# Products of the first thirteen blocks kept in a ring of four buffers, and the diagonal placed with a raised priority

## The chip, the cores and the metric

The kernel runs on one core of a Trainium2 chip. The metric is the time of one execution on the device in microseconds; the kernel before was run three times.

## The reference

A linear attention with a decaying state feeds two feed-forward layers. For every step t of 768, per batch (4) and head (8, of width 48):

```python
for t in range(S):
    kt, vt, rt = (k[:, :, t], v[:, :, t], r[:, :, t])
    cur = np.einsum('bhd,bhe->bhde', u[None] * kt, vt)
    y[:, :, t] = np.einsum('bhd,bhde->bhe', rt, state + cur)
    state = w[None, :, :, None] * state + np.einsum('bhd,bhe->bhde', kt, vt)
...
h = (x @ w1) * (x @ w2) @ w3          # first layer: x is 3072 x 384, inner width 1024
x = h @ w_out
h = x @ w_in                          # second layer: inner width 2048
return (h * np.cos(h)) @ w_out2
```

## The kernel before

The attention is done in 12 chunks of 64 steps. For chunk c and each half g of the heads, PE makes the scores `sc` (L518, L521), DVE puts them into the tile `am` under a strict mask (`mask_scores`, L533), ACT copies `am` into `xa` and `xb` (L539, L540), and PE multiplies these with the values to get `y` (L554) and the next state `st` (L591). ACT evacuates `y` to `yt` (L556); PE transposes it (`xp`, L569), and ACT and DVE split it into a high and a low half (`xh`, `xl`). Before the masks, DVE puts a diagonal into the same `am`: it forms the sums `dg` (L478, L480, L481) and places them with one predicated copy of 128x1024 (`prep_g`, L505). The scores of a chunk need its two operands `rd` and `kd`, which SP loads (L367) when the scores of the chunk before are done, and which DVE then scales in place (L486).

The first layer runs beside the attention. `ab(j, m)` makes, for a block of 512 tokens and 128 columns, `a = x @ w1` and `b = x @ w2`, each from nine products of high and low halves (`mm3`, L273 to L275). ACT copies `a` into an SBUF tile `p` (L772), DVE multiplies it by `b` (L773), and the POOL queue stores the product to DRAM, `pd` (L774); it is read back later. `a` and `b` lie in a ring of three PSUM banks, `p` in a ring of two SBUF buffers under the tag `p`. So the copy for a block waits until the store of an earlier block has left its buffer.

Another ring, tag `stg`, has four buffers of the same size. Its first user is `hot`, the operand of the filler products `hps` (L409) that stop before the 35th microsecond. The next ones are the pieces of w3 that `fold_load` splits (two buffers for each pair of steps, with `FOLD` from block 14 on), later the staged x2 and the output.

The weights come as 64-bit numbers; `decode` turns them into high and low halves on DVE (L313, L316, L319, L332) and ACT (L330).

A scheduler orders the instructions of each engine by priority, by data and by when a buffer comes free. The order is fixed when the program is built, and each engine then runs its own list in that order. `tc.high_priority(offset=40)` puts what stands under it 40 places ahead; the masks have it in `att_mask`, and the copy and the multiplication of `p` have -80.

```python
BUFS = {"wx": 4, "wf": 4, "p": 2, "ph": 3, "pl": 3, "stg": 4, "raw": 2, "dt": 1}
ORDER = [(j, m) for j, a, b in ((0, 0, 6), (1, 0, 4), (0, 6, 8), (1, 4, 8)) for m in range(a, b)]
FOLD = [0] * 14 + [1, 1, 1, 0] * 8 + [0] * 2
```

Of the kernel before, what the change touches and what calls it, by code (L numbers as in the profile page):

```python
# [184 lines left out]
def kernel(  # L185
# [19 lines left out]
    with ExitStack() as own:  # L205
        held = own.enter_context(tc.tile_pool(name="held", bufs=1))
        dram = own.enter_context(tc.tile_pool(name="slow", bufs=1, space=DRAM))
        flag = held.tile([1, 1], I32, name="flag")
        chunked(
            tc, flag, rd_in, kd_in, rt_in, kt_in, vt_in, wT_in, u_in, w1_in, w2_in, w3T_in, wo_in, wi2_in, wo2_in, out  # L210
        )
        odd = nc.values_load(flag[0:1, 0:1], min_val=0, max_val=48)
        with tc.If(odd > 0):
            xc = dram.tile([out.shape[0], 384, 512], F32, name="xc")
            sequential(tc, rt_in, kt_in, vt_in, w_in, u_in, xc)
            plain(tc, xc, w1_in, w2_in, w3T_in, wo_in, wi2_in, wo2_in, out)
# [3 lines left out]
def chunked(  # L220
# [41 lines left out]
    def kt_(tag, shape, nm, dt=F32):  # L262
        return keep.tile(list(shape), dt, tag=tag, name=nm, bufs=BUFS[tag])

    def bank(nm, tag):
        return psum.tile([128, 512], F32, tag=tag, name=nm, bufs={"ab": 3, "att": 2, "acc": 3}[tag])
# [5 lines left out]
    def mm3(o, wh, wl, xh, xl, first, last):  # L272
        nc.tensor.matmul(o, wh, xh, start=first, stop=False)  # L273
        nc.tensor.matmul(o, wh, xl, start=False, stop=False)  # L274
        nc.tensor.matmul(o, wl, xh, start=False, stop=last)  # L275
# [7 lines left out]
    def flush():  # L283
        while late:
            late.pop(0)()
# [204 lines left out]
    def masked(c):  # L490
        return ((ams[c], 0, 128),)
# [9 lines left out]
            nc.scalar.copy(zb[0:64], kt[0:64])  # L501

    def prep_g(c):
        for x, o, e in masked(c):
            nc.vector.copy_predicated(  # L505
                out=x[o:e].rearrange("p g h t -> p (g h) t"),
                mask=mdiag[o:e].unsqueeze(1).to_broadcast([e - o, 2 * H, C]),
                data=dg[o:e].unsqueeze(2).to_broadcast([e - o, 2 * H, C]),
            )
# [87 lines left out]
    halves, whole = [slice(0, 256), slice(256, 512)], slice(0, 512)  # L597
# [6 lines left out]
    def att_slot(c, i):  # L604
        if c >= NSTEP:
            return
        n = c + 1 if c + 1 < NSTEP else None
        if i == 0:
            att_scores(c)
            att_mask(c)  # L610
            loads(c + 1)
        elif i == 1:
            att_y(c, 0)
            att_state(c, 0)
            if n:
                prep_d(n)
        elif i == 2:
            att_y(c, 1)
            att_x(c, 0)
            att_state(c, 1)  # L620
            if n:
                load_v(n)
                prep_u(n)
        else:
            att_x(c, 1)
            if n:
                prep_z(n)
                prep_g(n)
# [10 lines left out]
    def w12(m, n):  # L639
        g, i = divmod(m, 4)  # L640
        fs = slice(i * 128, (i + n) * 128)
        for which, hi, lo in ((1, w1h, w1l), (2, w2h, w2l)):
            if g not in hi:
                hi[g] = wp.tile([128, 3, 512], F32R, tag=f"g{g}", bufs=4, name=f"w{which}h{g}")
                lo[g] = wp.tile([128, 3, 512], F32R, tag=f"g{g}", bufs=4, name=f"w{which}l{g}")
            decode(w12_id[which, m], (hi[g][:, :, fs], lo[g][:, :, fs]))
# [6 lines left out]
    for ps in range(3):  # L653
        n = 128 * min(3, NM1 - 3 * ps)
# [42 lines left out]
    def fold_step(n):  # L697
        for _ in range(n):
            if folds:
                it = folds.pop(0)  # L700
                fold_load(*it)
                fold_pend.append(it)
            if len(fold_pend) > (2 if folds else 0):
                if not folds:
                    flush()
                fold_mm(*fold_pend.pop(0))
# [48 lines left out]
                nc.scalar.copy(s, acc[j][e])  # L755
                nc.sync.dma_start(out=x2d[j][:, e, :], in_=s)

    def ab(j, m, cols=slice(0, 512)):
        g, i = divmod(m, 4)
        fs = slice(i * 128, (i + 1) * 128)  # L760
        n = cols.stop - cols.start
        a = bank(f"a{j}_{m}", "ab")[:, 0:n]
        b = bank(f"b{j}_{m}", "ab")[:, 0:n]
        for t, wh, wl in ((a, w1h, w1l), (b, w2h, w2l)):
            for kk in range(3):
                mm3(
                    t, wh[g][:, kk, fs], wl[g][:, kk, fs], xh[j][:, kk, cols], xl[j][:, kk, cols], kk == 0, kk == 2
                )
        p = kt_("p", (128, 512), f"p{j}_{m}")[:, 0:n]

        with tc.high_priority(offset=-80):
            nc.scalar.copy(p, a)  # L772
            nc.vector.tensor_tensor(out=p, in0=p, in1=b, op=ALU.mult)  # L773
        nc.gpsimd.dma_start(out=pd[j][m][:, cols], in_=p)  # L774
# [28 lines left out]
    load_v(1)  # L803
    prep_u(0)
    prep_g(0)
    att_mask(0)
    warm(24)
# [10 lines left out]
    decays()  # L818
    flush()
    ab(0, 0, halves[0])  # L820
    prep_u(1)
    prep_g(1)
    prep_z(1)
    att_mask(1)
# [5 lines left out]
    att_state(1, 0)  # L830
    flush()
    ab(0, 1, halves[0])
    att_x(1, 1)
    att_state(1, 1)
# [11 lines left out]
    def advance(n):  # L846
        for _ in range(n):
            att_slot(*next(slots, (NSTEP, 0)))

    for i, (j, m) in enumerate(ORDER):  # L850
        advance(SLOTS[i])
        if i in (1, 6):
            w12({1: 4, 6: 6}[i], 2)
        fold_step(FOLD[i])
        flush()
        ab(j, m, halves[1] if j == 0 and m < 2 else whole)
    while folds or fold_pend:
        fold_step(1)
    att_cm.__exit__(None, None, None)
# [16 lines left out]
    for i in range(NBLK * NM1):  # L876
        j, m = divmod(i, NM1)
# [64 lines left out]
    for it in items + [None] * 5:  # L942
        if it:
            j, m = it
# [80 lines left out]
```

## Time and profile before

| | us |
|---|---|
| median of three runs | 863.75 |
| the three runs | 861.83, 863.75, 864.93 |
| the profiled execution, its own time | 865.14 |
| its span (first to last instruction) | 863.4 |
| PE busy in the span | 840.5 (97%) |
| DVE busy | 554.8 (64%) |
| ACT busy | 415.6 (48%) |

The execution has 1.74 us outside of its span. PE is the busiest engine; how its idle time lies in the span is told by the waits and by the busy times in stretches. A granted clock of 1.00 is full speed, 2.4 GHz, and 0.50 is 1.2 GHz.

### The profile page before, as it was taken

The page shows a single profiled execution, that of the slowest core. Times are in us where ns is not written, and L with a number is a line of the kernel's source. Part 1 is how long each engine was busy: PE and PEld are TensorE (multiplying, and loading weights), DVE is VectorE, ACT ScalarE, POOL GpSimd, SP SyncE. Part 2 cuts the span into 40 slices and gives each one's busy share as a digit, 9 for nine tenths or more (in the row PEclk, how much of TensorE's full clock was granted, in tenths as well). Part 3 has the DMA queues.
Part 4 walks back from the last instruction along what each step waited for, and adds up shares of the span by engine and source line. Part 5 has one row for each costly group of instructions (what it writes and reads, how often), then busy time and mean ns, then how long its engine had stood idle before and what let it go on. Part 6 is the DMA issues. An engine that isn't in the chain of part 4 may idle for free.

```text
span 863.4 us, 14166 instructions
## 1 busy us (share of the span) xinstructions
PE 840.5 (97%) x5630; PEld 682.9 (79%) x5634; DVE 554.8 (64%) x839; ACT 415.6 (48%) x708; POOL 35.9 (4%) x66
## 2 busy tenths in 40 slices
PE   6987999999999999999999999999999999999997
PEld 3775778888888888888888888888888888888885
DVE  8876977786555534498956655655655655655552
ACT  4764555544553531255446445445545544544442
POOL 3000010010100001000000000000000000000000
PEclk9988999999999999999999999999999999999998
DMA  8757566565343263288952002001001100100101
GB/s 254 208 182 221 163 199 210 177 206 151 113 149 110 71 209 132 90 305 296 326 177 74 1 1 73 1 1 59 15 1 38 36 0 15 59 0 1 38 1 40
DMA packets 41161, 95.04 MB, mean 110 GB/s; under 512 B 4736, under 2 KB 6400, under 8 KB 41088
## 3 DMA queue, kind: packets, MB, share of 16 engines
q1 hardware_dynamic: 37072, 81.28, 30.0%
q0 software_dynamic: 3872, 12.59, 3.9%
q8 instruction: 46, 0.75, 0.4%
q10 hardware_dynamic: 144, 0.20, 0.1%
q14 instruction: 27, 0.22, 0.1%
HBM read 72.03 MB, written 22.02 MB: 109 GB/s over the span
## 4 chain that ended last, share of the span: by engine, by line
PE 94%; DVE 2%; DMA 1%; ACT 1%; issue 1%; ACTq 0%; DVEq 0%
PE p L274 12%; PE p L273 12%; PE p L275 12%; PE h L275 8%; PE h L273 8%; PE h L274 8%; PE a L273 4%; PE b L273 4%; PE b L275 4%; PE b L274 4%; PE a L274 4%; PE a L275 4%; PE y L554 3%; PE sc L518 2%; PE hps L409 2%; PE st L591 2%
## 5 line engine op out<-in xcount | busy, mean ns | idle before, releaser
L921 ACT ACTIVATE u<-h,qbias 128x512 f32<-128x512 f32 x96 | 66.2, 689 | 138.0 <-PE h L275 138.0
L922 DVE TENSOR_SCALAR n<-u 128x512 f32<-128x512 f32 x96 | 41.1, 428 | 138.0 <-ACT u L921 138.0
L275 PE MATMUL h<-x2h,wil 128*128 128x512 f32 x288 | 113.2, 393 | 0.0
L273 PE MATMUL h<-x2h,wih 128*128 128x512 f32 x288 | 113.1, 393 | 0.0
L274 PE MATMUL p<-gl,woh 128*128 128x512 f32 x288 | 113.1, 393 | 0.0
L274 PE MATMUL h<-x2l,wih 128*128 128x512 f32 x288 | 113.0, 392 | 0.0
L275 PE MATMUL p<-gh,wol 128*128 128x512 f32 x288 | 113.0, 392 | 0.0
L273 PE MATMUL p<-gh,woh 128*128 128x512 f32 x288 | 113.0, 392 | 0.0
L924 ACT ACTIVATE u<-n 128x512 f32<-128x512 f32 x96 | 60.9, 634 | 65.1 <-DVE n L923 65.1
L930 DVE TENSOR_TENSOR u<-u,h 128x512 f32<-128x512 f32 x96 | 66.0, 687 | 16.7 <-ACT u L924 16.7
L773 DVE TENSOR_TENSOR p<-p,b 128x512 f32<-128x512 f32 (+1 forms) x50 | 33.1, 661 | 62.4 <-PE b L275 35.7
L923 DVE SCALAR_TENSOR_TENSOR n<-n,u 128x512 f32<-128x512 f32 x96 | 66.4, 692 | 3.3
L936 DVE TENSOR_TENSOR gl<-u,gh 128x512 fp32r<-128x512 f32 x96 | 65.7, 685 | 0.7 <-ACT gh L932 0.7
L274 PEld LDWEIGHTS p<-gl,woh 128*128 128x128 f32 x288 | 54.1, 188 | 12.4
L275 PEld LDWEIGHTS h<-x2h,wil 128*128 128x128 f32 x288 | 54.1, 188 | 12.3
L273 PEld LDWEIGHTS h<-x2h,wih 128*128 128x128 f32 x288 | 54.1, 188 | 12.3
L274 PEld LDWEIGHTS h<-x2l,wih 128*128 128x128 f32 x288 | 54.1, 188 | 12.2
L273 PEld LDWEIGHTS p<-gh,woh 128*128 128x128 f32 x288 | 54.1, 188 | 12.2
L275 PEld LDWEIGHTS p<-gh,wol 128*128 128x128 f32 x288 | 54.1, 188 | 12.2
L772 ACT COPY p<-a 128x512 f32<-128x512 f32 (+1 forms) x50 | 28.3, 568 | 67.3 <-PE a L275 56.0
L273 PE MATMUL a<-xh,w1h 128*128 128x512 f32 (+1 forms) x150 | 60.4, 403 | 0.0
L932 ACT CAST gh<-u 128x512 fp32r<-128x512 f32 x96 | 58.9, 613 | 0.8 <-DVE u L930 0.8
(163 smaller groups left out, 1717.5 us busy)
## 6 DMA issues: line engine op xcount, KB each, us to landing
pr<-pd SPq DMA_DIRECT2D x48, 256.0 KB, 4.1
pd<-p POOLq DMA_DIRECT2D x46, 256.0 KB, 2.8
raw<-in_wo_dram SPq DMA_DIRECT2D x12, 768.0 KB, 5.0
raw<-in_w3T_dram SPq DMA_DIRECT2D x8, 768.0 KB, 5.0
raw<-in_wi_dram SPq DMA_DIRECT2D x8, 768.0 KB, 5.6
raw<-in_w_dram SPq DMA_DIRECT2D x6, 768.0 KB, 5.7
x2d<-x SPq DMA_DIRECT2D x18, 256.0 KB, 5.5
x2s<-x2d SPq DMA_DIRECT2D x18, 256.0 KB, 3.3
```

What stands on the lines that cost most here:

```text
L273: nc.tensor.matmul(o, wh, xh, start=first, stop=False)
L274: nc.tensor.matmul(o, wh, xl, start=False, stop=False)
L275: nc.tensor.matmul(o, wl, xh, start=False, stop=last)
L772: nc.scalar.copy(p, a)
L773: nc.vector.tensor_tensor(out=p, in0=p, in1=b, op=ALU.mult)
L921: head[0] = nc.scalar.activation(out=u, in_=h, func=AF.Identity, scale=INV_2PI, bias=qbias).ins
L922: nc.vector.tensor_scalar_add(out=n, in0=u, scalar1=RND)
L923: nc.vector.scalar_tensor_tensor(out=n, in0=n, scalar=RND, in1=u, op0=ALU.subtract, op1=ALU.subtract)
L924: nc.scalar.activation(out=u, in_=n, func=AF.Sin, scale=-TWO_PI)
L930: nc.vector.tensor_tensor(out=u, in0=u, in1=h, op=ALU.mult)
L932: nc.scalar.copy(gh, u)
L936: nc.vector.tensor_tensor(out=gl, in0=u, in1=gh.bitcast(F32), op=ALU.subtract)
```

## The change

The diagonal's placement gets the priority that the masks behind it have, and the products of the half blocks ahead of the loop and of the loop's first 13 blocks (i from 0 to 12) are kept in the ring `stg` and no more in `p`.

```diff
     def prep_g(c):
+        with tc.high_priority(offset=40):
+            place_diagonal(c)
+
+    def place_diagonal(c):
         for x, o, e in masked(c):
             nc.vector.copy_predicated(
...
-    def ab(j, m, cols=slice(0, 512)):
+    def ab(j, m, cols=slice(0, 512), early=True):
...
-        p = kt_("p", (128, 512), f"p{j}_{m}")[:, 0:n]
+        p = kt_("stg" if early else "p", (128, 512), f"p{j}_{m}")[:, 0:n]
...
-        ab(j, m, halves[1] if j == 0 and m < 2 else whole)
+        ab(j, m, halves[1] if j == 0 and m < 2 else whole, early=i < 13)
```

No instruction is added or left out. What moves is the order on PE, DVE, ACT and SP; on POOL nothing moves. In the names below, `y2_0` is the y of chunk 2, first half of the heads, `b0_1` the b of block j = 0, m = 1; a number behind that is the buffer's. Line numbers of the changed kernel are four higher from `prep_g`'s body on.

On DVE, where chunk 2 is prepared, the kernel before has:

```order
L496 TENSOR_TENSOR kt_130<-kt_130,tk0_139 128x768
L332 TENSOR_TENSOR w1l0_362<-dt4_678,w1h0_361 128x3x256
L505 COPY_PREDICATED am_133<-mdiag_143,dg_144 128x1024
L313 TENSOR_SCALAR dt5_686<-raw5_593 128x768
L533 COPY_PREDICATED am_133<-mstrict_142,sc2_0_705 128x512
L316 SCALAR_TENSOR_TENSOR dt5_686<-raw5_593,dt5_686 128x768
L533 COPY_PREDICATED am_133<-mstrict_142,sc2_1_722 128x512
```

And the changed kernel:

```order
L496 TENSOR_TENSOR kt_130<-kt_130,tk0_139 128x768
L509 COPY_PREDICATED am_133<-mdiag_143,dg_144 128x1024
L332 TENSOR_TENSOR w1l0_362<-dt4_678,w1h0_361 128x3x256
L537 COPY_PREDICATED am_133<-mstrict_142,sc2_0_705 128x512
L313 TENSOR_SCALAR dt5_686<-raw5_593 128x768
L537 COPY_PREDICATED am_133<-mstrict_142,sc2_1_722 128x512
L316 SCALAR_TENSOR_TENSOR dt5_686<-raw5_593,dt5_686 128x768
```

The diagonal has passed the low half of w1, and each of the two masks one step of the next decoding.

On PE at the same place, the changed kernel has the end of `a0_1`, then the nine products of `b0_1`, and then `y2_0` (in the kernel before, `b0_1` stands behind the 32 products of `y2_0` and `st2_0`, 32 rows further on):

```order
L275 MATMUL a0_1_835<-xh0_380,w1l0_362 128x256
L273 MATMUL b0_1_836<-xh0_380,w2h0_370 128x256
L274 MATMUL b0_1_836<-xl0_381,w2h0_370 128x256
L275 MATMUL b0_1_836<-xh0_380,w2l0_371 128x256
...
L558 MATMUL y2_0_775<-va_134,xa_131 64x48
L595 MATMUL st2_0_794<-va_134,za_136 48x48
L558 MATMUL y2_0_775<-vb_135,xb_132 64x48
```

So PE has nine products to do where it stood before `y2_0`.

On ACT, where chunk 3 is worked on, the kernel before has:

```order
L500 COPY za_136<-kt_130 64x768
L501 COPY zb_137<-kt_130 64x768
L539 COPY xa_131<-am_133 64x512
L540 COPY xb_132<-am_133 64x512
L539 COPY xa_131<-am_133 64x512
L540 COPY xb_132<-am_133 64x512
L772 COPY p0_4_1076<-a0_4_1056 128x512
L556 COPY yt3_0_1033<-y3_0_1016 128x384
```

And the changed kernel:

```order
L776 COPY p0_4_1076<-a0_4_1056 128x512
L500 COPY za_136<-kt_130 64x768
L501 COPY zb_137<-kt_130 64x768
L543 COPY xa_131<-am_133 64x512
L544 COPY xb_132<-am_133 64x512
L543 COPY xa_131<-am_133 64x512
L544 COPY xb_132<-am_133 64x512
L560 COPY yt3_0_1033<-y3_0_1016 128x384
```

The copy of the product `p0_4` no more stands between the masked scores and the evacuation of `y3_0`.

On PE, a little later, the changed kernel has the scores of chunk 4 behind the first product of `a1_0` and of `b1_0` (before, behind all of `a1_0`, `b1_0`, `a1_1` and `b1_1`):

```order
L573 MATMUL xp3_1_1129<-ident_141,yt3_1_1097 128x128 x3
L273 MATMUL b0_5_1142<-xh0_380,w2h1_824 128x512
L274 MATMUL b0_5_1142<-xl0_381,w2h1_824 128x512
L275 MATMUL b0_5_1142<-xh0_380,w2l1_825 128x512
L273 MATMUL a1_0_1181<-xh1_878,w1h0_361 128x512
L273 MATMUL b1_0_1182<-xh1_878,w2h0_370 128x512
L522 MATMUL sc4_0_1229<-rd_127,kd_128 64x64
L525 MATMUL sc4_0_1229<-rd_127,kd_128 64x64
```

The scores of chunk 4 have passed 34 products of the first layer.

## Rows read from the trace of the kernel before

**Rows 1.** Busy time by stretch: length, engines' busy us, PE clock, DMA share, GB/s.

```profile
48.20:51.00 2.80, 0.03 (x1) 0.03 (x1) 2.80 (x5) 1.31 (x3) 0.00 (x0) 0.84 1.05 307
51.00:57.00 6.00, 5.80 (x75) 5.33 (x75) 6.00 (x10) 3.85 (x7) 1.08 (x2) 0.51 0.63 187
57.00:78.20 21.20, 20.91 (x253) 16.07 (x252) 16.49 (x22) 11.54 (x18) 1.62 (x3) 1.00 0.68 203
78.20:83.60 5.40, 0.06 (x3) 0.03 (x2) 1.66 (x2) 1.05 (x3) 0.00 (x0) 0.74 0.87 294
83.60:88.00 4.40, 4.40 (x56) 3.56 (x58) 1.35 (x3) 3.48 (x6) 0.54 (x1) 0.54 0.18 67
88.00:111.00 23.00, 23.00 (x177) 18.72 (x172) 21.53 (x27) 10.28 (x16) 2.16 (x4) 1.00 0.65 184
111.00:857.00 746.00, 746.00 (x4495) 610.33 (x4493) 462.55 (x709) 353.44 (x596) 21.77 (x39) 1.00 0.29 96
```

**Rows 2.** Waits of PE, 20 to 120 us: total, times, longest.

```profile
PE y L554 <- ACT yt L556: 5.3, 1, 5.3
PE y L554 <- DMA rd<-in_rd_dram: 2.8, 1, 2.8
```

**Rows 3.** Chain that ended last: start, us, what.

```profile
73.99 8.48 DMA pd<-p
...
83.57 1.95 PE y L554 x32
...
111.54 1.07 PE y L554 x32
112.61 0.72 PE st L591 x32
...
122.99 0.48 PE xp L569 x3
```

**Rows 4.** ACT in order of time: start, us, form; in brackets idle before, releaser.

```profile
50.30 0.61 ACT L539 COPY xa<-am 64x512 f32<-64x512 f32 x1 [1.47 <-DVE am L533]
50.95 0.62 ACT L540 COPY xb<-am 64x512 f32<-64x512 f32 x1
...
82.55 0.58 ACT L772 COPY p<-a 128x512 f32<-128x512 f32 x1 [5.57 <-DMA pd<-p]
83.03 0.48 ACT L556 COPY yt<-y 128x384 f32<-128x384 f32 x1
```

**Rows 5.** DVE in order of time.

```profile
46.99 0.95 DVE L332 TENSOR_TENSOR w1l<-dt,w1h 128x768 fp32r<-128x768 f32 x1
47.86 1.29 DVE L505 COPY_PREDICATED am<-mdiag,dg 128x1024 f32<-128x1024 uint8 x1
49.04 0.55 DVE L313 TENSOR_SCALAR dt<-raw 128x768 uint32<-128x768 uint32 x1
49.50 0.71 DVE L533 COPY_PREDICATED am<-mstrict,sc 128x512 f32<-128x512 uint8 x1
...
79.66 1.23 DVE L486 TENSOR_TENSOR rd<-rd,t 128x1024 f32<-128x1024 f32 x1 [1.68 <-DMA rd<-in_rd_dram]
```

**Rows 6.** PE in order of time.

```profile
51.62 0.34 PE L554 MATMUL y<-vb,xb 112*64 112x48 f32 x1 [0.20 <-ACT xb L540]
...
89.58 0.39 PE L273 MATMUL a<-xh,w1h 128*128 128x512 f32 x1
...
98.67 0.40 PE L273 MATMUL b<-xh,w2h 128*128 128x512 f32 x1
```

**Rows 7.** POOL's issue of the third store of a product.

```profile
55.49 0.54 POOL L774 DMA_DIRECT2D pd<-p  x1 [1.78 <-DVE p L773]
```

**Rows 8.** The loads of rd: SP's issue, their landing, and the median of all.

```profile
71.94 0.79 SPq L367 DMA_DIRECT2D rd<-in_rd_dram  x2
...
DMA to landing us min/median/max: 6.4/6.8/7.2
...
rd<-in_rd_dram SPq DMA_DIRECT2D x20, 192.0 KB, 4.4
```

## The prediction

> **What bounds the kernel now.** I read the busy times by stretch first, then PE's waits, then the chain of waits backwards, and last the lists of ACT and DVE at the two places that the waits name. The stretches [rows 1] show that from 111 to 857 us PE is busy for 746.00 of 746.00 us at a clock of 1.00: whatever PE gets done earlier before 111 us arrives whole at the end, and nothing else does. Ahead of that, two stretches are nearly empty, 48.2 to 51 (0.03 us busy) and 78.2 to 83.6 (0.06), and behind each lies one at about half clock (0.51 and 0.54). PE's waits name them [rows 2]: 2.8 us and 5.3 us, both before products `y`.
>
> The longer one ends in the chain with 8.48 us of a store `pd` issued at 73.99, and PE's `y` starts at 83.57 [rows 3]. ACT tells why [rows 4]: at 82.55 it copies a product after 5.57 us of waiting for that store, and the evacuation `yt`, for which PE waits, is the next one in its list, at 83.03. The `y` that it evacuates was done long before. So a two-buffer ring of products stops the attention, only because ACT works in order.
>
> The shorter one is put down to a load of `rd`. But ACT's copies into `xa` and `xb` at 50.30 and 50.95 wait for DVE's mask [rows 4], and DVE works without a pause there: it is busy 2.80 of 2.80 us [rows 1]. So DVE's order is the cause: the diagonal starts only at 47.86, behind a low half of w1 at 46.99, and the mask at 49.50, behind a decoding step at 49.04 [rows 5].
>
> **The change, part by part.** The sum is made against the profiled execution: 863.4 us of span and 1.74 around it, 865.14.
>
> *The first pause.* With the diagonal first, DVE goes diagonal, low half, mask. The diagonal starts at 46.99; it takes 49.04 - 47.86 = 1.18 to the next start, the low half 47.86 - 46.99 = 0.87, so the first mask starts at 49.04 and no more at 49.50 [rows 5]. `xb` and then the run of `y` products follow 0.46 us earlier: 51.16 for 51.62 [rows 6]. What is late next is that copy again. In the pause PE now also has the nine products of `b0_1`, which it did later before; 39 products of 512 columns follow each other from 89.58 to 98.67, 0.233 us apiece [rows 6], so one of 256 columns takes about half, 0.117, and nine 1.05. They wait for ACT's copy of `a0_1`, 0.37 us that goes into the 1.47 us in which ACT sat idle before 50.30 [rows 4]. Gain: 0.46 + 1.05 = 1.5 us. The low half of w1 comes 1.2 us later; the block that wants it begins only behind `y2_1`, some 4 us on, so it costs nothing, and without that cover 1.2 us.
>
> *The clock behind it.* From 51 to 57 us PE was busy 5.80 of 6.00 us with a clock of 0.51 [rows 1]: half of what it did there would have taken half the time. At 1.00 that saves 5.80/2 = 2.9 us. The pause of 2.8 us, whole and empty, becomes two shorter ones of about 1 us each with products between. The trace shows a fall in each of the two empty stretches (clock 0.84 and 0.74 over them) and none elsewhere ahead of the end, so a broken pause is shown by no row. Bounds: 0 (it falls all the same) and 2.9; I take 2.9, since the PE is never empty for as long as in either row.
>
> What the Trainium skill says in TensorE: Matmul & The Clock Gate, section What's actually happening, speaks for care here: activity releases a throttled default, and the window over which it is judged runs free of the program. By that, where the fall comes may differ between executions; the traced two do not contradict it, and with a fall the sum would be 2.9 us smaller.
>
> *The second pause.* The ring `stg` has four buffers, and the copy of `p0_4` waits for the store of four products earlier, the one issued at 55.49 [rows 7], and no more for the one at 73.99. In the new order it also stands ahead of `za` and the masked scores and not in front of `yt`. So both what made it wait and what it blocked are gone: 5.3 us [rows 2]. What is late next is ACT's list of four copies of `am`, which ends before PE arrives. Behind the pause the clock was 0.54 for 4.40 busy us [rows 1]; low share (1 - 0.54)/0.5 = 0.92, so 4.40 x 0.92 / 2 = 2.0 us come back. Bounds for this pair: 5.3 (another fall) and 7.3; I take 7.3.
>
> *What the new order adds.* The scores of chunk 4 pass 34 products and now wait, on PE, for `rd` and `kd` of that chunk, with the rest of `a1_0` and `b1_0` queued behind them. SP loads these once the scores of chunk 3 are done. Up to there PE is 1.5 + 2.9 = 4.4 us earlier, but does 15 more products first (seven of `a0_4`, four of `b0_4`, four of `a0_5`). At 0.233 us these are 3.5 us; the loads go out 0.9 us earlier than 71.94, near 71.0. If they land after 6.8 us as before [rows 8], DVE scales `rd` at 78.8 for 79.66 [rows 5], and `kd` behind four other steps: with a 1.2 us scaling at either end and 0.95, 0.56, 0.55 and 0.95 between, near 84. PE from 71.0 has 21 products (4.9 us), two `y`, two `st` and two `xp` (2 x 1.07 + 2 x 0.72 + 2 x 0.48 = 4.5 [rows 3]) and arrives at 80.4: 3.6 us of waiting. Landing in the median 4.4 us of all such loads [rows 8] takes 2.4 off: 1.2. These are the bounds; I take 2.5, between them, since the next weights are now fetched well ahead of these loads and no more directly in front.
>
> *Nothing else.* The later products go back to the two-buffer ring; PE never waited there after 111 us [rows 1]. The pieces of w3, which share `stg`, need it from block 14 on. DVE must keep up: from 48.2 to 111 it is busy 49.8 of 62.8 us [rows 1] in sum, so 13 us is the most that PE can gain there, and 9 leave it 4.
>
> Sum: 1.5 + 2.9 + 7.3 - 2.5 = 9.2 us. 865.14 - 9.2 = 855.9. The median of the three runs is 1.39 below the profiled one, so a median comes to 854.6.
>
> **The rivals.**
>
> *The clock falls all the same* at the first pause. For: in the 3.2 us from 48 on PE does barely 1.1 us of work. Against: never 2 us empty in one piece. Price 2.9 us: 857.5. Chance 0.17.
>
> *The loads of chunk 4 become the new wait.* Products are stored earlier: those of `p0_3` and `p0_4` (256 KB each) fall near 72 to 73 us, on top of the loads of `rd`, in a stretch in which the DMA engines are at 0.87 already and move 294 GB/s [rows 1]: 512 KB take 1.8 us. PE then waits 2.5 + 1.8 = 4.3 us, about 2 of them at one go or more, and a fall of the clock is due, 2.0 us as at the second pause. 854.6 + 3.8 = 858.4. For it speaks DVE's 1.68 us of waiting for these very loads [rows 5], against it that the stores are no more waited for, so only the loads matter. Chance 0.19. The Trainium skill, DMA: Bandwidth & Descriptors, section Queues, rings and completion order, says that each DMA engine takes turns between the queues by packets; that speaks for this rival, as a store on POOL's queue would not stand behind SP's loads but slow them, and by it the sum would be 1.8 us smaller; the 8.48 us of one store of 256 KB between such loads fits.
>
> *The pause stays under another name*: PE waits before chunk 3's `y` for something else for as long, its masks or weights. DVE's 16.49 of 21.20 us busy before it [rows 1] leaves room, which speaks against it. Then only 4.4 us are gained: 859.4. Chance 0.05.
>
> *Slower.* The pieces of w3 share the ring with the products, and ACT converts them in order: if a conversion stands in ACT's list before a `yt` and its buffer waits for a store, the whole second pause returns there, 7.3 us each. One costs most of the gain (861.9); with two it is 869, so from the second on it is slower. Against: from 111 us on PE runs without a pause, and w3 begins when the stores have had several blocks of 4 us to land. Chance 0.03, and 0.01 for no change in all.
>
> **How the numbers follow.** 0.55 is left for 854.6. Differences under 0.3%, 2.6 us, can't be told from none here: the three runs lie 3.1 us apart. All cases but the last two are faster than that: that is 0.96, of which 0.03 go to the middle for cases that mix; so faster 0.93, same 0.04, slower 0.03. The range goes from 851, where the waits for chunk 4 all but vanish (2.5) and the runs lie a us lower, to 859.5, which takes in the rivals of 857.5, 858.4 and 859.4.
>
> **What would show it.** Right: no wait of PE for `yt` over 1 us; `y` of chunk 2 starting near 51.2 and a clock of 1.00 from 48 to 88 us; DVE's diagonal directly behind 46.1 us' scaling of `kt`; ACT's waits for `pd` gone before 100 us; a wait of PE of 1.2 to 3.6 us shortly before `a1_0`. Wrong: a clock of 0.5 behind 50 us, a wait for `rd` over 4 us near 80 us, or any pause of PE after 111 us less the gain.

## The result, and the profile after

The changed kernel takes 854.96 us (median of 6 runs, 854.02 to 855.62); the kernel before, run beside it, 863.54 (6 runs, 861.83 to 864.93). The ratio is 0.9901, interval 0.9888 to 0.9914: 8.6 us faster, where 854.6 was forecast. The profiled execution took 855.62 us with a span of 853.9.

The three longest of PE's waits from 20 to 130 us in the changed kernel (total, times, longest):

```profile
PE b L273 <- ACT p L776: 1.0, 1, 1.0
PE xp L573 <- DVE xl L579: 0.6, 1, 0.6
PE b L273 <- ACT w2h L330: 0.3, 1, 0.3
```

Both long waits of [rows 2] are gone; the 0.6 was in the kernel before too, ahead of the first pause. Now the busy times by stretch (length; busy us of PE, PE's loads, DVE, ACT, POOL; PE clock, DMA share, GB/s):

```profile
48.20:51.50 3.30, 2.57 (x35) 2.14 (x37) 3.30 (x6) 2.45 (x6) 0.00 (x0) 1.00 1.00 273
51.50:57.00 5.50, 5.50 (x121) 4.80 (x117) 5.17 (x8) 5.19 (x10) 1.08 (x2) 1.00 0.65 206
79.00:84.00 5.00, 5.00 (x50) 3.72 (x49) 5.00 (x7) 2.53 (x5) 0.00 (x0) 1.00 0.65 203
84.00:90.00 6.00, 6.00 (x32) 4.58 (x32) 6.00 (x9) 3.82 (x6) 0.64 (x2) 1.00 0.64 178
```

Against [rows 1], the stretch behind 51 us has a clock of 1.00 for 0.51, and the empty one near 80 us is full. DVE at the first pause, start and duration:

```profile
45.76 0.95 DVE L496 TENSOR_TENSOR kt<-kt,tk 128x768 f32<-128x768 f32 x1
46.63 1.32 DVE L509 COPY_PREDICATED am<-mdiag,dg 128x1024 f32<-128x1024 uint8 x1
47.83 0.95 DVE L332 TENSOR_TENSOR w1l<-dt,w1h 128x768 fp32r<-128x768 f32 x1
48.69 0.75 DVE L537 COPY_PREDICATED am<-mstrict,sc 128x512 f32<-128x512 uint8 x1
```

and what PE does with it:

```profile
48.80 0.38 PE L273 MATMUL b<-xh,w2h 128*128 128x256 f32 x1 [1.04 <-ACT p L776]
50.20 0.32 PE L558 MATMUL y<-va,xa 128*64 128x48 f32 x2
50.85 0.26 PE L558 MATMUL y<-va,xa 128*64 128x48 f32 x1
```

The order is that foreseen: scaling, diagonal, low half, mask. Against [rows 5] the diagonal comes 1.2 us earlier. PE waits 1.04 us for ACT's copy of `a0_1`, does the nine products of `b0_1`, and is in the run of `y` at 50.85 where it was at 51.62 [rows 6].

ACT where the second pause was:

```profile
67.54 0.58 ACT L776 COPY p<-a 128x512 f32<-128x512 f32 x1
70.24 0.83 ACT L500 COPY za<-kt 64x768 f32<-64x768 f32 x1 [2.13 <-issue]
...
74.50 0.48 ACT L560 COPY yt<-y 128x384 f32<-128x384 f32 x1
```

The copy of `p0_4` waits for nothing and lies ahead of the masked scores; `yt` follows 8.5 us earlier than in [rows 4]. In the chain of waits, the landmarks that answer to [rows 3]:

```profile
53.58 8.21 DMA rt<-in_rt_dram
...
75.38 1.07 PE y L558 x32
...
100.53 1.07 PE y L558 x32
```

The `y` of chunk 3's second half takes 1.07 us for 1.95 (full clock) and starts 8.2 us earlier; the next `y` starts at 100.53 for 111.54, 11.0 us earlier. PE's last product starts at 845.72 for 856.70 before, also 11.0. The span is only 9.5 us shorter: from that product to the end it is 8.19 us here and 6.72 before, and SP's last three stores were issued over 3.38 us here and over 1.73 before. Over all twelve traces this end takes 6.7 to 8.2 us, in the kernel before too 6.7 to 7.7.

### The profile page after: what moved, and what is told of

Its sections match the earlier page's. It is cut to its first block, busy times and chain, and to the rows that moved or that the text cites. A ratio compares the mean times of both kernels' runs of the same rounds, so it can differ in the third digit from the quotient of the medians.

```text
span 853.9 us, 14167 instructions
## 1 busy us (share of the span) xinstructions
PE 836.7 (98%) x5630; PEld 679.1 (80%) x5634; DVE 554.8 (65%) x839; ACT 415.3 (49%) x708; POOL 35.1 (4%) x66
## 4 chain that ended last, share of the span: by engine, by line
PE 95%; DMA 2%; DVE 1%; ACT 1%; issue 0%; SPq 0%; DVEq 0%; ACTq 0%
PE p L274 12%; PE p L273 12%; PE p L275 12%; PE h L275 8%; PE h L273 8%; PE h L274 8%; PE a L273 4%; PE b L273 4%; PE b L275 4%; PE b L274 4%; PE a L274 4%; PE a L275 4%; PE y L558 3%; PE sc L522 2%; PE hps L409 2%; PE st L595 2%
## 5 line engine op out<-in xcount | busy, mean ns | idle before, releaser
L273 PE MATMUL b<-xh,w2h 128*128 128x512 f32 (+1 forms) x150 | 58.3, 389 | 1.3 <-ACT p L776 1.0
```

## Experiments

The start of the stretch that is changed and the stores behind the last product vary between executions, so the traces are compared by the time from DVE's scaling of `kt` (L496, near 46 us) to the start of PE's last product. "Low clock" is the time at 0.50 between 45 and 100 us, read in steps of half a us. Except for the first two rows, each of these two columns rests on one trace.

| kernel | median us | ratio to before (interval) | L496 to last product, us | low clock, us |
|---|---|---|---|---|
| before, three traces | 863.5 to 864.5 | 1 | 810.58, 809.50, 809.37 | 13.7, 10.3, 10.2 |
| changed, two traces | 854.96; 854.33 | 0.9901; 0.9888 | 799.96, 800.18 | 0, 0 |
| ring alone | 855.92 | 0.9899 (0.9878 to 0.992) | 801.25 | 0 |
| diagonal alone | 858.37 | 0.9931 (0.991 to 0.9953) | 804.51 | 3.4 |
| one product in `stg` alone | 857.93 | 0.9921 (0.9899 to 0.9943) | 802.04 | 0 |
| diagonal and that product | 858.84 | 0.9946 (0.9924 to 0.9967) | 804.1 | 0 |
| fillers in the first pause | 863.92 | 0.9998 (0.9982 to 1.0014) | 809.51 | 6.8 |
| all products in `stg` | 859.56 | 0.9952 (0.9935 to 0.9969) | 805.5 | 0 |
| changed, copies of halves earlier | 854.30 | 0.9891 (0.9871 to 0.991) | the scaling itself moved | 0 |

**The diagonal alone.** All products stay in `p`; only `prep_g` is changed.

```diff
     def prep_g(c):
+        with tc.high_priority(offset=40):
+            place_diagonal(c)
+
+    def place_diagonal(c):
```

> Only the diagonal gets the raised priority; all products stay in the ring of two buffers. In the order that this gives, the first pause has no products of b0_1 in it, and the multiplication of p0_2 stands ahead of the low half of w1 as in the changed kernel, near 60 us where it was at 73.04. Theory A, the ring alone takes the second pause away: p0_4's copy still waits for the store of p0_2 and blocks ACT, PE stands still for about 5 us near 70 to 80 us, the gain is 0.5 us and the median 863. Theory B, the new order is enough: the store of p0_2 goes out near 61 us, 13 us earlier than before, and even a landing of 8.5 us is over before p0_4's copy is due near 68; the second pause is gone (7.3 us), the first one is 2.4 us long and the clock may fall behind it, so the gain is 7 to 8 us without and 10 us with a clock that holds: 853.5 to 856.5.

ACT, start, duration and what it had waited for:

```profile
64.67 0.59 ACT L776 COPY p<-a 128x512 f32<-128x512 f32 x1 [2.74 <-DMA pd<-p]
...
69.03 0.58 ACT L776 COPY p<-a 128x512 f32<-128x512 f32 x1 [0.62 <-PE a L275]
...
96.44 0.58 ACT L776 COPY p<-a 128x512 f32<-128x512 f32 x1 [5.10 <-DMA pd<-p]
```

and PE's waits from 40 to 130 us:

```profile
PE y L558 <- ACT xa L543: 2.3, 1, 2.3
PE b L273 <- ACT p L776: 1.7, 1, 1.7
```

The second pause is gone without the ring: with the order changed upstream, the product whose store ACT waited for in [rows 4] is multiplied and stored some 12 us earlier. The first pause is shorter by 0.5 us and empty, with 3.4 us of low clock behind it, and a store of the two-buffer ring now stops PE at 97 us. So theory B had the mechanism, but 858.37 lies above its 853.5 to 856.5.

**The ring alone.** The changed kernel without the diagonal's priority.

```diff
     def prep_g(c):
-        with tc.high_priority(offset=40):
-            place_diagonal(c)
+        place_diagonal(c)
```

> Only the ring of four buffers for the early products; the diagonal keeps its place behind the low half of w1. Theory A (ring and order both matter): the second pause is gone (7.3 us), the first pause still ends at 51.6 us but has the nine products of b0_1 in it, and the clock holds there: gain 7.3 + 1.05 + 2.9 = 11 us less a few tenths of new waits, 852.5 to 854. Theory B (it takes the earlier masks to keep the clock): the granted clock is 0.5 somewhere from 50 to 57 us, and the gain is 8 us, 855.5. If the diagonal is what takes the second pause away, PE waits 5 us for yt near 80 us again and the gain is 1 to 4 us, 860 or more.

```profile
PE b L273 <- ACT p L775: 0.9, 1, 0.9
PE xp L572 <- DVE xl L578: 0.6, 1, 0.6
PE y L557 <- ACT xa L542: 0.5, 1, 0.5
PE y L557 <- ACT xb L543: 0.3, 1, 0.3
```

These are its waits from 20 to 130 us. The clock does not fall, and yet 855.92 lies above the 852.5 to 854 of theory A. The first pause is three short waits (without the `xp`), 0.7 us more than in the changed kernel: two of them are for the copies of the mask, which comes later. So the ring brings most of the gain, and the diagonal 1.2 us on top in the traces (801.25 against 800.07, the mean of two); in the times against before this is not clear of the noise (0.9899 against 0.9901 and 0.9888).

**One product.** The kernel before, with only `p0_4` in `stg`.

```diff
-        ab(j, m, halves[1] if j == 0 and m < 2 else whole)
+        ab(j, m, halves[1] if j == 0 and m < 2 else whole, early=i == 4)
```

> The kernel before with one edit: of all products only p0_4 (block i = 4) is kept in the ring of four buffers, so its copy waits for no store. PE's order is that of before but for a product or two. Theory A, one product's buffer makes the whole second pause: PE's wait of 5.3 us for yt is gone, the clock holds from 57 us on, the first pause and its low clock stay: gain 7.3 us, 856.2. Theory B, the pause is handed on: DVE's order or the loads of chunk 4 (landing at 79.6) hold PE a few us later instead, or the clock falls there all the same: gain 2 to 5 us, 858.5 to 861.5.

ACT behind 72 us, and PE's longest wait and the stretch of the first pause:

```profile
72.75 0.58 ACT L772 COPY p<-a 128x512 f32<-128x512 f32 x1 [0.58 <-PE a L275]
...
76.72 0.48 ACT L556 COPY yt<-y 128x384 f32<-128x384 f32 x1 [0.38 <-PE y L554]
```

```profile
PE y L554 <- DMA rd<-in_rd_dram: 3.0, 1, 3.0
50.50:54.00 3.50, 1.33 (x38) 1.21 (x40) 3.50 (x7) 2.06 (x4) 0.00 (x0) 1.00 0.81 180
54.00:57.50 3.50, 3.50 (x80) 3.26 (x76) 3.21 (x6) 2.70 (x6) 0.80 (x2) 1.00 0.69 172
```

One buffer takes the second pause away: the cause named in the prediction holds. The time, 857.93, is above the 856.2 of theory A. The first pause is 3.0 us here, the longest of all, and yet the clock behind it is 1.00, where I expected the low clock to stay. With the second pause and its fall gone, the chain has the two `y` that answer to 83.57 and 111.54 in [rows 3]:

```profile
77.80 1.07 PE y L554 x32
...
104.37 1.07 PE y L554 x32
```

That is 26.57 us for the same products that took 27.97 with the fall: 1.4 us is the price of the second fall in the first trace of before (1.8 and 1.4 in the two others below), for the 2.0 of the sum.

**Two more traces of the kernel before and one of the changed kernel**, without an edit, to see what of [rows 1 and 2] belongs to the one execution.

> The kernel before, profiled once more. Theory A, what an execution pays for the clock differs from one to the next: pauses of 2.3 us and 2.8 us were followed by half clock in two traces, one of 3.0 us in a third one was not. Then one of the two falls, most likely the one behind the shorter first pause, can be missing here, the pauses themselves stay at 2 to 3 and 5 to 6 us, and from DVE's scaling of kt (L496, near 46 us) to PE's last product it takes 807 to 811 us. Theory B, the clock falls behind every pause of over 2.3 us in this place and the third trace was an exception by its other order: both falls are there again and the stretch is 810.6 us.

> The kernel before, profiled a third time, for the same question. Theory A: the fall behind the first pause is missing in one of the two at least, the stretch from L496 to the last product is then 2 to 3 us shorter. Theory B: both falls again, 810.6 us.

> The changed kernel once more, profiled and timed. No pause of PE over 1.1 us from 40 to 840 us and a granted clock of 1.00 all through, as in its first trace; from L496 to PE's last product 800.0 us within 0.5; the rest of the span (start, and last store, whose issue took 3.38 us in the first trace and 1.73 us in all others) differs by 1 to 2 us. The median is 8 to 9 us under that of before.

The stretch behind the first pause in the second trace of before:

```profile
51.00:57.00 6.00, 5.67 (x105) 5.23 (x105) 6.00 (x9) 3.67 (x7) 1.08 (x2) 0.72 0.72 203
```

The pauses are 2.69 and 4.7, 2.70 and 4.8 us, like the first trace's, but in both the clock is 0.72 for 0.51: half as long at the lower level. In both the first pause is put down to ACT's copy `xa`, as the prediction read it, and not to the load of `rd`. The second fall is the same in all three (6.8 us). So neither theory holds as it stood: no fall is missing, but the first one differs in length, and the stretch to the last product is 1.1 to 1.2 us shorter. The changed kernel is without a fall ahead of 100 us in both of its traces, as foreseen.

**Fillers in the first pause.** The kernel before with 13 products on a constant tile, whose result nothing reads, nine of them right ahead of `a0_1`.

```diff
+    def fill_pause(n):
+        hp2 = bank("hp2", "acc")
+        for _ in range(n):
+            nc.tensor.matmul(hp2, hot[:, 0:128], hot, start=True, stop=True)
...
+            if c == 2:
+                fill_pause(13)
```

> The kernel before with 13 filler products (128x512, bf16, nothing reads their result): nine of them stand right ahead of a0_1, four a little earlier where PE has short waits, so that PE is not empty for nearly 3 us ahead of y2_0. They keep the first pause's end where it is (DVE's masks) and only shorten its empty part by about 2 us. Theory A, the half clock behind the pause costs what it shows: the clock stays at 1.00 from 48 to 58 us, PE is done 2.9 us earlier, the second pause stays: gain 2 to 3 us, 860.5 to 861.5. Theory B, DVE, busy without a break from 48 to 57 us, is what PE would wait for at full clock: gain under 1 us, 863. Theory C, four fillers outside of the pause cost more than the clock brings: 864.

PE's start of `y2_0`, of chunk 3's scores, and the stretch behind the pause; then the same two starts in the second trace of before:

```profile
50.33 0.32 PE L554 MATMUL y<-va,xa 128*64 128x48 f32 x2 [0.72 <-DMA rd<-in_rd_dram]
59.22 0.27 PE L518 MATMUL sc<-rd,kd 48*64 48x64 f32 x1
51.00:57.00 6.00, 6.00 (x114) 5.21 (x116) 5.75 (x9) 5.00 (x9) 1.08 (x2) 1.00 0.66 202
```

```profile
50.89 0.32 PE L554 MATMUL y<-va,xa 128*64 128x48 f32 x2 [2.69 <-ACT xa L539]
61.25 0.27 PE L518 MATMUL sc<-rd,kd 48*64 48x64 f32 x1
```

and in the first trace of before:

```profile
50.97 0.34 PE L554 MATMUL y<-va,xa 128*64 128x48 f32 x1 [2.84 <-DMA rd<-in_rd_dram]
62.22 0.27 PE L518 MATMUL sc<-rd,kd 48*64 48x64 f32 x1
```

This gives the price of the first fall, since PE does the same products between these two points: 8.89 us at full clock (8.89 also with one product in `stg`, from 52.34 to 61.23), 10.36 in the second trace (clock 0.72), and 11.25 in the first (0.51). So 1.5 and 2.4 us. But the time does not change: theory A's gain of 2 to 3 us did not come. POOL's and ACT's lists at the second pause:

```profile
71.38 0.54 POOL L781 DMA_DIRECT2D pd<-p  x1 [10.53 <-DVE p L780]
```

```profile
80.27 0.58 ACT L779 COPY p<-a 128x512 f32<-128x512 f32 x1 [5.91 <-DMA pd<-p]
80.75 0.49 ACT L556 COPY yt<-y 128x384 f32<-128x384 f32 x1
```

Counted from the scaling of `kt`, the store is issued 1.1 us earlier than in the two other traces of before (25.92 for 27.00 and 27.04), but the copy comes 8.89 us behind it, for 7.95 and 8.04 there. PE waits 5.7 us for 4.7 and 4.8, and of the 1.5 us that were won at the scores 0.1 to 0.3 are left at the `y` behind the pause (35.83 for 35.96 and 36.10). So the gain ahead of the second pause was swallowed by the landing of that store. It was not alone in this: the load of `kt` that SP issues 0.6 us before it landed 34.52 us behind the scaling here and 34.54 and 34.67 there, although it was issued 1.5 us earlier. Why these transfers end no earlier stays open; with one product in `stg` the same store, issued at 25.88, landed a us earlier.

**The diagonal and one product.** The two above put together; the other products stay in the ring of two.

```diff
-    def ab(j, m, cols=slice(0, 512), early=True):
+    def ab(j, m, cols=slice(0, 512), early=False):
...
-        ab(j, m, halves[1] if j == 0 and m < 2 else whole, early=i < 13)
+        ab(j, m, halves[1] if j == 0 and m < 2 else whole, early=i == 4)
```

> The kernel before with the diagonal's raised priority and only one product, that of block (0, 4), kept in stg; the other products stay in the ring of two. So b0_1 stands behind y2_0 again, and the pause ahead of y2_0 is one empty piece of about 2.3 us as with the diagonal alone. If the gain is the diagonal (about 1.1 us), the second pause (about 5.3 and the clock behind it 2.0) and the products in the first pause (about 1), and the other products in stg give nothing, it lies 1 to 3 us above the changed kernel: 855.5 to 857.5, ratio 0.991 to 0.994, with or without a low clock behind 50 us; no wait of ACT for a store ahead of 100 us. If the ring's use by the later products matters too, a wait like the 1.67 us at 97 us of the kernel with the diagonal alone is there again and it comes out at 858 or more, ratio 0.994.

PE's waits from 40 to 130 us:

```profile
PE y L558 <- ACT xa L543: 2.3, 1, 2.3
PE a L273 <- ACT p L776: 1.4, 2, 1.2
PE b L273 <- ACT p L776: 1.1, 1, 1.1
```

The later products in `stg` matter. The 1.2 (at 61.9 us) and the 1.1 (at 97.3 us) stand behind copies that wait 2.61 and 4.58 us for stores of the two-buffer ring, at places where no store stopped PE in the kernel before. That PE meets them because it is earlier is my reading. With the 2.3 and a last one of 0.2 the waits come to 5.0 us for 1.3 in the changed kernel: 3.7 more, and the stretch is 4.0 us longer. I had 855.5 to 857.5 for the one theory and 858 or more for the other: the second holds.

**All products in `stg`.** The test of the rival for slower.

```diff
-        ab(j, m, halves[1] if j == 0 and m < 2 else whole, early=i < 13)
+        ab(j, m, halves[1] if j == 0 and m < 2 else whole, early=True)
```

> The changed kernel with the products of all blocks in the ring stg, none in p. From block 14 on they share its four buffers with the pieces of w3 and w4. This puts the price of the rival for slower to the test. My theory: nothing changes ahead of 88 us, and behind it PE gets no longer waits because the stores land several blocks before their buffer is wanted: ratio to the kernel before 0.988 to 0.992, PE's waits from 111 us to its last product under 1 us in sum, last product near 845.5. The rival: conversions of w3 pieces and copies of products wait for each other in ACT's list, and PE stands still for some us, once per block of the fold at worst: with one pause of 5 us the last product comes at 850.5 and the ratio is 0.995; with 7.3 us for each of two or more it is above 1.00.

DVE, then ACT and then PE near 173 us, where PE of the changed kernel goes on without a wait:

```profile
168.46 0.56 DVE L332 TENSOR_TENSOR w3l<-dt,w3h 128x384 fp32r<-128x384 f32 x1 [1.92 <-DMA pd<-p]
...
170.26 0.74 DVE L537 COPY_PREDICATED am<-mstrict,sc 128x512 f32<-128x512 uint8 x1
```

```profile
171.09 0.62 ACT L543 COPY xa<-am 64x512 f32<-64x512 f32 x1 [7.38 <-DVE am L537]
...
173.75 0.57 ACT L776 COPY p<-a 128x512 f32<-128x512 f32 x1
```

```profile
174.37 0.50 PE L273 MATMUL b<-xh,w2h 128*128 128x512 f32 x1 [1.47 <-ACT p L776]
```

My theory (no change behind 88 us) is wrong; the rival's mechanism exists, though it goes by DVE more than by ACT. A piece of w3 wants a buffer of `stg` whose store has not landed; DVE stands 1.92 us, the mask behind it is late, so `xa`, so the copy of the product, so PE. Waits of PE for such a copy come to 2.6 us behind 111 us (the next long one at 320 us, 1.0), and from the scaling to the last product it takes 5.4 us longer than in the changed kernel (mean of two traces); what makes up the other 2.8 us, no wait of the profile names. The bound of 13 blocks keeps the products out of that stretch.

**Copies of the half products earlier.** The changed kernel, with ACT's copy and DVE's multiplication of the 256-column products raised, against the 1.04 us ahead of `b0_1`.

```diff
-        with tc.high_priority(offset=-80):
+        with tc.high_priority(offset=-40 if n == 256 else -80):
```

> The changed kernel, and the copy and the multiplication of the half blocks have priority -40 where they had -80, so that ACT copies a0_1 before za and zb and before the masked scores. Theory A: PE's wait of 1.04 us ahead of b0_1 goes, the first pause is over when a0_2's first products, which now stand there too, are done: gain 0.5 to 1.5 us over the changed kernel, 853.5 to 854.5. Theory B: the masked scores and za come later by the copies' 0.37 us and 1.7 us, y2_0 with them, and the gain is given back: 855 to 856.

The wait ahead of `b0_1` is gone. PE waits for converted pieces of w2 (L330), 0.55 us at 39.7 and 0.51 at 68.0, where the changed kernel waits 0.57 for `xl` at 39.3 and 0.27 or 0.51 for w2 near 67.6. The last product starts at 845.36 for 845.54 and 845.72, and the time is 854.30 for 854.33, measured beside it: no gain, though 854.30 lies in theory A's range. DVE is busy throughout in this place (3.30 of 3.30 us in the changed kernel above), and the order shows what moved back: its scaling of `kt` is at 48.95 for 45.76.

## Why the prediction was right, step by step

The total was right by 0.4 us, and much of that is luck: a wait that was charged did not come, two terms for the clock were too large, and the end of the span, which the sum had at nothing, took 1.5 us in the profiled execution.

- **First pause, 1.5 us: right.** From the scaling of `kt` to the run of `y` it is 50.85 - 45.76 = 5.09 us for 51.62 - 46.12 = 5.50: 0.41 from the diagonal (0.46 was foreseen), with the 1.05 us of `b0_1` done in between. The ring alone lacks 1.2 us of the whole, more than 0.46; 0.7 of that are the two more waits of its `y`.
- **The clock behind it, 2.9 us: size off, mechanism supported and not shown.** A pause broken by products was followed by no fall in three traces (two of the changed kernel, one of the ring alone), and all 16 timed runs of these two kernels have a mean clock of 0.997 to 0.999; the traces without a fall ahead of 100 us have that too. But empty pauses of 2.27 and 2.97 us were followed by none either, so the products may not be what decides. And the term was read as half of the busy time in one trace; measured over the same work it is 2.4 us there and 1.5 us in the two other traces. The Trainium skill, TensorE: Matmul & The Clock Gate, section What's actually happening, says that the window over which activity is judged runs free of the program. The runs are in line with that: with the same order of work up to there, the same pause of 2.27 us was followed by a fall in one kernel (diagonal alone) and by none in another (diagonal and one product).
- **Second pause and its clock, 7.3 us: the pause right** (it was 4.7 to 5.3 us and is gone), **its clock too large** (1.4 us for 2.0), **incomplete in cause**. I gave the ring and the new order as one answer; either does it alone, the order by the diagonal alone, the ring by a single buffer.
- **Waits ahead of chunk 4's scores, -2.5 us: the step that failed.** The loads of `rd`, their landing, DVE's two scalings and PE's first score in the changed kernel:

```profile
70.98 0.79 SPq L367 DMA_DIRECT2D rd<-in_rd_dram  x2
DMA to landing us min/median/max: 4.1/4.2/4.3
75.76 1.23 DVE L486 TENSOR_TENSOR rd<-rd,t 128x1024 f32<-128x1024 f32 x1 [0.55 <-DMA rd<-in_rd_dram]
79.71 1.22 DVE L486 TENSOR_TENSOR kd<-kd,t 128x1024 f32<-128x1024 f32 x1
81.25 0.27 PE L522 MATMUL sc<-rd,kd 48*64 48x64 f32 x1
```

The loads were issued at 70.98, as worked out (71.0), but landed after 4.1 to 4.3 us and not after the 6.8 of [rows 8]. That 6.8 was itself one execution's: in the two other traces of before the same loads took 5.2 to 5.7 us. `kd` was done near 80.9; PE came to the scores at 81.25 (80.4 was foreseen) and waited for nothing. So even the lower bound of 1.2 us was too much. In place of this wait there is 0.3 us at 67.7, behind a conversion of w2 that the chain of waits leads back to a load of `rt` (8.21 us).
- **Nothing else: right** behind 111 us. The shift of 11.0 us is there at 100.53 (111.54 before [rows 3]) and at the last product.

With the measured sizes the sum for the two profiled executions is 1.5 + 2.4 + 6.7 - 0.3 = 10.3, against 810.58 - 799.96 = 10.6 from the scaling to the last product. Of the 11.0 us between the last products, 1.5 went to the end of the span.

How much of the whole is the clock's depends on what stands behind it. Of the 35 runs of the kernel before that were timed beside the experiments, six have a mean clock of 0.996 or 0.997, so at most a short fall ahead of the end (the trace with 3.4 us of low clock has 0.996). They took 862.7 us on the mean, the other 29 took 864.4. By this estimate the two falls together cost some 1.7 us as long as the pauses stay, and not 2.9 + 2.0: 1.4 for the second one, and little for the first, since the second pause takes back what is won ahead of it (with the fillers 0.1 to 0.3 us of 1.5 were left).

Of the rivals, the clock's fall did not come; the loads of chunk 4 were no wait; the pause under another name did not come. The rival for slower was rightly put behind the bound of 13 blocks: without that bound its mechanism takes back half of the gain (859.56), not all of it.

## What to carry to other kernels

Where one engine works in order, a copy that waits for a store stops everything listed behind it; look for that store, and for the next ones of the same ring, since with the first one gone later copies waited for stores that had stopped nothing before. A gain ahead of a pause that a transfer ends can be swallowed by that pause (as with the fillers), so take the last one first. Read the length of a fall and the landing of a load from more than one execution before you put them into a sum. A ring shared with a later stage is safe only up to where that stage begins to use it.

## What the runs showed of the hardware

- The same empty time does not always lower the clock. Falls came behind pauses of 2.27 (diagonal alone), 2.69, 2.70 and 2.84 us (the kernel before); none behind 2.27 us (diagonal and one product) and 2.97 us (one product), whose order of work up to there is that of the diagonal alone and of the kernel before. The time at 0.50 was 3.4 or 6.8 us in every fall of these traces ahead of 100 us.
- Work at the lower clock is not simply twice as long: a stretch of 8.89 us took 10.36 with 3.4 us of low clock in it, and 11.25 with 6.0.
- The same two loads of `rd`, 192 KB each, landed after 6.4 and 7.2 us in one execution of the kernel before and after 5.2 to 5.7 in two others; in the changed order it was 4.1 and 4.3, and 2.9 and 3.5 us. The spread is as large as the wait that was worked out from them [rows 8].
